# Last stage of an attention, expert and feed-forward kernel: accumulator bank by step, a lag of three, conversion in place, mixed pairs held in order

## The chip, the cores and the metric

The kernel runs on one core of a Trainium2 chip. The metric is the device time of one execution, in microseconds; the time before is the median of three runs, 920.2 us (919.64 to 920.55). One further execution was taken with the hardware profiler. Its rows name the engines PE (TensorE, matmuls), PEld (its weight loads), DVE (VectorE), ACT (ScalarE), POOL (GpSimd) and SP (SyncE, which issues most DMAs).

## The reference

Three layers follow each other on 2304 tokens of width 512. Cut to what matters:

```python
out = attention(q, k, v)                 # (4, 8, 576, 64): downsampled by 4, plus a local band of |i - j| < 4
x = out as (2304, 512)
e = argmax(x @ w_gate + bias[modality])  # one of 8 experts per token
x[e == k] = gate * (relu(x[e == k] @ w1[k]) @ w2[k])        # 512 -> 1024 -> 512
h = x @ w_in                             # 512 -> 2048
g = max(h, 0) + log1p(exp(-abs(h)))      # softplus
result = g @ w_out                       # 2048 -> 512
```

The large products need more than one pass: each operand is split into a high part (`h`) and the rest (`l`), and one product is three matmuls, high x high, high x low and low x high (`mm3`). The weights w_in and w_out arrive as 64-bit words and are converted on the chip first.

## The kernel before

Tokens are on 18 tiles of 128. After the attention, `slots` runs the experts: a slot is 128 tokens of one expert, and for each slot `gemm1` makes x @ w1, `h_t` transposes the hidden values (L1149) and splits them (L526 on ScalarE, L527 on VectorE), `gemm2` makes h @ w2. Slots 9 and 15 (of those executed) are mixed: their two halves of 64 tokens belong to two experts, and `mmx` (L561) issues for each weight slice two matmuls of half width, one for each half, with the weights `wh` and `wl` of the two experts. TensorE can run such a pair side by side. Weights come by DMA into the tiles raw0 to raw7, and ScalarE (L332) and VectorE (L333) split them.

The conversion of w_in and w_out lies beside this work. `conv_load` brings one half chunk, 512 KB, into the tile `cv` (two buffers, SyncE's queue, L188 for w_in and L191 for w_out). `conv_work` then makes 32-bit values: ScalarE scales the low words (L206, tile `cm`), VectorE shifts the high words into the tile `cy` (L209) and merges sign and the rest into `z` (L213), and GpSimd adds `cm` (L215). For the first eight chunks `z` is a tile `cz` and is stored to DRAM (`wf`), to be loaded again into a raw tile; for the last eight `z` is a half of raw4 to raw7 itself, and this runs in the last stage. `cm` and `cy` have two buffers in the slots and one in the last stage.

The last stage has 96 steps (g, c): six groups of three token tiles, sixteen chunks of 128 hidden columns. `ffn1` is the first product of a step, 12 matmuls (L552, L555, L556) into an accumulator bank `ps`, then the softplus: on ScalarE Abs (L1231, the first reader of the bank), Exp (L1232), 1 + e (L1234) and Ln (L1238), on VectorE L1237, L1239 (the last reader of the bank) and L1240, then gh (ScalarE, L1244) and gl (VectorE, L1245). `ffn2` is the second product, 9 matmuls of gh, gl with w_out into the three banks of its group, and runs LAG steps later in the program. `gather_y` (GpSimd, L1192) brings a token tile into `yg`, `y_t` transposes it (L1209), splits it (L527) and copies its index column into `ti` (VectorE, L1214).

Steps 0 to 15 are (0,0) to (0,7) and (1,0) to (1,7). Steps 16 to 21 are pairs of the two groups: (0,8), (1,8), (0,9), (1,9), (0,10), (1,10). Then (0,11) to (0,15), (1,11) to (1,15), and groups 2 to 5 in turn. The conversions of chunks 8 to 15 stand between steps 4 and 23.

The program is not executed in the order of the text: a planner with a model of the engines sets the order of every engine's queue, and only instructions marked `keep_in_program_order` keep their order among each other. Every engine works through its queue in order, each instruction behind the waits for its inputs and for free buffers.

Of the kernel before, what the change touches and what calls it, by code (L numbers as in the profile page):

```python
# [11 lines left out]
I32 = mybir.dt.int32  # L12
# [7 lines left out]
def tile_attention_moe_ffn(  # L20
# [17 lines left out]
    NT, DM = out.shape  # L38
# [31 lines left out]
    NFC = FF // 128  # L70
# [17 lines left out]
    def bank(i, shape, dt=F32):  # L88
        return psums[-1].tile(shape, dt, tag=f"p{i}", name=f"p{i}")
# [86 lines left out]
    cvp = []  # L176
# [19 lines left out]
    def conv_work():  # L196
        if cvl:
# [6 lines left out]
            m = cvp[-1].tile([128, DM], I32, tag="cm", name="cm")  # L204
            y = cvp[-1].tile([128, DM], I32, tag="cy", name="cy")
            i1 = act.activation(out=m, in_=low.bitcast(U32), func=ACTF.Copy, scale=2.0 ** -29)  # L206
            if c >= CD:
                tc.keep_in_program_order(i1)
            i1 = dve.tensor_scalar(out=y, in0=h, scalar1=3, scalar2=0x3FFFFFFF,  # L209
                              op0=ALU.logical_shift_left, op1=ALU.bitwise_and)  # L210
            if c >= CD:
                tc.keep_in_program_order(i1)
            dve.scalar_tensor_tensor(out=z, in0=h, scalar=-0x40000000, in1=y,  # L213
                                     op0=ALU.bitwise_and, op1=ALU.bitwise_or)
# [342 lines left out]

    def mmx(ps, L, R, first, last):
        for a in range(2):
            ph = slice(64 * a, 64 * a + 64)  # L560
            pe.matmul(out=ps[ph], lhsT=L[:, ph], rhs=R[a], start=first, stop=last)  # L561

# [570 lines left out]
    def phase_cd():  # L1133
# [4 lines left out]
        fpl = []  # L1138
# [37 lines left out]
        OB = 2  # L1176
        GB = 4
        GN = GT * 128
# [40 lines left out]

        def ffn1(g, c):  # L1220
            yh, yl = yT[g]
            wh, wl = split[FF0 + c]
            ps = bank(c % 2, [128, GN])
            for kc in range(KC):
# [15 lines left out]
            dve.tensor_tensor(out=e, in0=e, in1=u, op=ALU.add)  # L1240
            gp = (fpl[1], GB) if g == len(groups) - 1 and c >= NFC - GB else (fp, 3)
            gh = gp[0].tile([128, GN], F32R, tag="gh", name="gh", bufs=gp[1])
# [122 lines left out]
        for f in acts[-1]:  # L1365
            f()
        LAG = 2
        LAST = 6
        for i in range(len(steps) + LAG):
            if i < len(steps):  # L1370
                early_ = i < 4 * CD - 4
                if not early_:
                    for f in acts[i]:
                        f()
                ffn1(*steps[i])
                if early_:
                    for f in acts[i]:
                        f()
# [48 lines left out]
```

## Time and profile before

| | |
|---|---|
| median of three runs | 920.2 us |
| the profiled execution | 925.12 us, of which its span 923.4 us |
| TensorE busy | 853.3 us, 92% of the span |
| VectorE busy | 654.7 us, 71% |
| ScalarE busy | 547.1 us, 59% |
| GpSimd busy | 214.8 us, 23% |

The attention ends at about 205 us, the slots at about 490 us, and the last stage fills the rest. The share of TensorE is a mean over these: in most of the last stage it is busy without a break, and the idle time sits in the attention, at the seam to the last stage, and in single waits. So the timeline has to be read by stage, and for each wait the bracket at the end of its row says how long the engine stood and what ended it.

### The profile page before, as it was taken

Reading aid. Unit: us, or ns where it says so; the run is one execution under the profiler, and the core shown is the slowest. Engines: PE = TensorE matmul, PEld = TensorE weight load, DVE = VectorE, ACT = ScalarE, POOL = GpSimd, SP = SyncE. Lnnn points to the kernel's source line nnn. Section 1 sums busy time; section 2 is a strip of 40 time slices with the busy share of each in tenths; the row PEclk is TensorE's granted clock in tenths of the full one; section 3 lists DMA queues with packets and bytes.
Section 4 is the critical chain, followed back from the end, with each engine's and each line's share of the span. In section 5 each row is a group of like instructions: output and inputs, shape, how many; then the busy total and the mean of one; then the engine's idle time right before and its main releaser. Section 6 shows DMA issues by size and latency. Waiting matters only on the chain. (4 is left out here: it accounts for less than half of the span.)

```text
span 923.4 us, 15325 instructions
## 1 busy us (share of the span) xinstructions
PE 853.3 (92%) x5356; PEld 725.9 (79%) x5356; DVE 654.7 (71%) x1271; ACT 547.1 (59%) x935; POOL 214.8 (23%) x263
## 2 busy tenths in 40 slices
PE   6797899868899999999999999899999999999996
PEld 6687788756777766786687898789899998999984
DVE  6576487678699988976857798656656665666662
ACT  3553564453699777876857677656545555455451
POOL 8322554230243342511001222202000000000001
PEclk9998899799999999999999999999999999999999
DMA  9999785672934599577354333202001001000000
GB/s 164 191 174 195 171 199 126 177 194 94 309 123 138 175 368 332 205 265 252 115 194 147 99 94 109 69 12 65 27 12 35 23 12 34 24 12 12 24 1 34
DMA packets 109112, 115.68 MB, mean 125 GB/s; under 512 B 68448, under 2 KB 83552, under 8 KB 109024
## 3 DMA queue, kind: packets, MB, share of 16 engines
q1 hardware_dynamic: 101072, 98.28, 38.0%
q0 software_dynamic: 4960, 16.28, 5.5%
q8 instruction: 44, 0.72, 0.3%
q10 hardware_dynamic: 2992, 0.04, 0.2%
q14 instruction: 44, 0.36, 0.1%
HBM read 92.93 MB, written 21.65 MB: 124 GB/s over the span
## 5 line engine op out<-in xcount | busy, mean ns | idle before, releaser
L333 DVE TENSOR_TENSOR wl<-raw,wh 128x1024 fp32r<-128x1024 f32 x152 | 187.6, 1256 | 34.8 <-ACT wh L332 31.8
L332 ACT ACTIVATE wh<-raw 128x1024 fp32r<-128x1024 f32 x152 | 159.2, 1064 | 39.8 <-DMA raw<-in_moe_w_dram 16.7
L552 PE MATMUL p<-yh,wh 128*128 128x384 f32 x384 | 131.6, 343 | 11.3 <-DVE e L1239 10.1
L556 PE MATMUL p<-yh,wl 128*128 128x384 f32 x384 | 129.4, 337 | 0.0
L555 PE MATMUL p<-yl,wh 128*128 128x384 f32 x384 | 129.3, 337 | 0.0
L552 PE MATMUL p<-wh,gh 128*128 128x512 f32 x288 | 113.8, 395 | 1.1 <-ACT gh L1244 1.1
L555 PE MATMUL p<-wl,gh 128*128 128x512 f32 x288 | 113.2, 393 | 0.0
L556 PE MATMUL p<-wh,gl 128*128 128x512 f32 x288 | 101.4, 395 | 0.1
L1238 ACT ACTIVATE u<-u 128x384 f32<-128x384 f32 x96 | 50.1, 524 | 80.1 <-DVE e L1237 80.1
L552 PEld LDWEIGHTS p<-yh,wh 128*128 128x128 f32 x384 | 72.1, 188 | 18.7 <-DVE e L1239 14.2
L1245 DVE TENSOR_TENSOR gl<-e,gh 128x384 fp32r<-128x384 f32 x96 | 57.5, 600 | 40.7 <-ACT gh L1244 39.9
L1244 ACT ACTIVATE gh<-e 128x384 fp32r<-128x384 f32 x96 | 50.1, 523 | 45.1 <-DVE e L1240 44.8
L555 PEld LDWEIGHTS p<-yl,wh 128*128 128x128 f32 x384 | 72.2, 188 | 3.0
L1231 ACT ACTIVATE e<-p 128x384 f32<-128x384 f32 x96 | 46.4, 488 | 46.3 <-PE p L556 42.8
L556 PEld LDWEIGHTS p<-yh,wl 128*128 128x128 f32 x384 | 72.1, 188 | 0.3
L1192 POOL DMA_INDIRECT yg<-ys,pos x18 | 19.1, 1060 | 216.4 <-PE p L1209 205.7
L1237 DVE SCALAR_TENSOR_TENSOR e<-u,e 128x384 f32<-128x384 f32 x96 | 55.2, 577 | 13.4 <-ACT u L1234 11.2
L556 PEld LDWEIGHTS p<-wh,gl 128*128 128x128 f32 x288 | 54.0, 188 | 12.9 <-DVE gl L1245 0.8
L552 PEld LDWEIGHTS p<-wh,gh 128*128 128x128 f32 x288 | 54.1, 188 | 10.5 <-ACT gh L1244 1.5
L1240 DVE TENSOR_TENSOR e<-e,u 128x384 f32<-128x384 f32 x96 | 55.3, 579 | 9.0 <-ACT u L1238 1.3
L555 PEld LDWEIGHTS p<-wl,gh 128*128 128x128 f32 x288 | 54.2, 188 | 8.7
L552 PE MATMUL p<-wh,hh 128*128 128x512 f32 x144 | 58.9, 409 | 1.8 <-ACT y L1170 1.5
(256 smaller groups left out, 1800.4 us busy)
## 6 DMA issues: line engine op xcount, KB each, us to landing
raw<-in_moe_w_dram SPq DMA_DIRECT2D x40, 512.0 KB
cv<-in_moe_w_in_dram SPq DMA_DIRECT2D x16, 512.0 KB
cv<-in_moe_w_out_dram SPq DMA_DIRECT2D x16, 512.0 KB
wh<-in_moe_w_dram SPq DMA_DIRECT2D x16, 512.0 KB
wl<-in_moe_w_dram SPq DMA_DIRECT2D x16, 512.0 KB
vw<-in_v_dram SPq DMA_DIRECT2D x36, 144.0 KB
ys<-y SPq DMA_DIRECT2D x20, 256.5 KB
vg<-in_v_dram SPq DMA_DIRECT2D x16, 288.0 KB
```

Of the source, the lines that this page charges most:

```text
L332: ins = (act.activation(out=hi, in_=r, func=ACTF.Copy), dve.tensor_tensor(out=lo, in0=r, in1=f32(hi), op=ALU.subtract))
L333: dve.tensor_tensor(out=lo, in0=r, in1=f32(hi), op=ALU.subtract))
L552: i = pe.matmul(out=ps, lhsT=lh, rhs=rh, start=first, stop=False)
L555: pe.matmul(out=ps, lhsT=lh, rhs=rl, start=False, stop=False)
L556: pe.matmul(out=ps, lhsT=ll, rhs=rh, start=False, stop=last)
L1192: pool.indirect_dma_start(out=y, out_offset=None, in_=ys[0:rows], in_offset=bass.IndirectOffsetOnAxis(ap=pos[:, t:t + 1], axis=0))
L1231: act.activation(out=e, in_=ps, func=ACTF.Abs)
L1237: dve.scalar_tensor_tensor(out=e, in0=u, scalar=-1.0, in1=e, op0=ALU.add, op1=ALU.subtract)
L1238: act.activation(out=u, in_=u, func=ACTF.Ln)
L1240: dve.tensor_tensor(out=e, in0=e, in1=u, op=ALU.add)
L1244: act.activation(out=gh, in_=e, func=ACTF.Copy)
L1245: dve.tensor_tensor(out=gl, in0=e, in1=f32(gh), op=ALU.subtract)
```

## The change

There are four edits. The first product's bank is i % 2 with i the number of the step, where it was c % 2; the two differ only in some of steps 17 to 26. LAG is 3, where it was 2, with gh and gl in four buffers (were three), and GB is 3 (was 4), the number of last steps whose gh and gl have their own pool. In `conv_work` the tile `cy` is gone: the shifted high words are written straight into `z`, and the merge reads `z` and writes it. In `mmx` the half-width matmuls are marked to keep the program's order.

```diff
--- before.py
+++ after.py
@@ -202,15 +202,14 @@
             else:
                 z = raws[4 + c % 4][:, j * DM:(j + 1) * DM].bitcast(I32)
             m = cvp[-1].tile([128, DM], I32, tag="cm", name="cm")
-            y = cvp[-1].tile([128, DM], I32, tag="cy", name="cy")
             i1 = act.activation(out=m, in_=low.bitcast(U32), func=ACTF.Copy, scale=2.0 ** -29)
             if c >= CD:
                 tc.keep_in_program_order(i1)
-            i1 = dve.tensor_scalar(out=y, in0=h, scalar1=3, scalar2=0x3FFFFFFF,
+            i1 = dve.tensor_scalar(out=z, in0=h, scalar1=3, scalar2=0x3FFFFFFF,
                               op0=ALU.logical_shift_left, op1=ALU.bitwise_and)
             if c >= CD:
                 tc.keep_in_program_order(i1)
-            dve.scalar_tensor_tensor(out=z, in0=h, scalar=-0x40000000, in1=y,
+            dve.scalar_tensor_tensor(out=z, in0=h, scalar=-0x40000000, in1=z,
                                      op0=ALU.bitwise_and, op1=ALU.bitwise_or)
             pool.tensor_tensor(out=z, in0=z, in1=m, op=ALU.add)
             if c < CD:
@@ -556,9 +555,10 @@
         pe.matmul(out=ps, lhsT=ll, rhs=rh, start=False, stop=last)
 
     def mmx(ps, L, R, first, last):
+
         for a in range(2):
             ph = slice(64 * a, 64 * a + 64)
-            pe.matmul(out=ps[ph], lhsT=L[:, ph], rhs=R[a], start=first, stop=last)
+            tc.keep_in_program_order(pe.matmul(out=ps[ph], lhsT=L[:, ph], rhs=R[a], start=first, stop=last))
 
     def gemm1(s):
         for _ in gemm1_steps(s):
@@ -1174,7 +1174,7 @@
 
         GT = 3
         OB = 2
-        GB = 4
+        GB = 3
         GN = GT * 128
         groups = [list(range(t, t + GT)) for t in range(0, NTT, GT)]
 
@@ -1217,10 +1217,10 @@
         def acc(g):
             return 2 + 3 * (g % 2)
 
-        def ffn1(g, c):
+        def ffn1(i, g, c):
             yh, yl = yT[g]
             wh, wl = split[FF0 + c]
-            ps = bank(c % 2, [128, GN])
+            ps = bank(i % 2, [128, GN])
             for kc in range(KC):
                 sl = slice(kc * 128, (kc + 1) * 128)
                 mm3(ps, (wh[:, sl], wl[:, sl]), (yh[:, kc, :], yl[:, kc, :]), kc == 0, kc == KC - 1)
@@ -1238,7 +1238,7 @@
             act.activation(out=u, in_=u, func=ACTF.Ln)
             dve.scalar_tensor_tensor(out=e, in0=ps, scalar=0.0, in1=e, op0=ALU.max, op1=ALU.subtract)
             dve.tensor_tensor(out=e, in0=e, in1=u, op=ALU.add)
-            gp = (fpl[1], GB) if g == len(groups) - 1 and c >= NFC - GB else (fp, 3)
+            gp = (fpl[1], GB) if g == len(groups) - 1 and c >= NFC - GB else (fp, 4)
             gh = gp[0].tile([128, GN], F32R, tag="gh", name="gh", bufs=gp[1])
             gl = gp[0].tile([128, GN], F32R, tag="gl", name="gl", bufs=gp[1])
             act.activation(out=gh, in_=e, func=ACTF.Copy)
@@ -1364,7 +1364,7 @@
                 acts[at + 1].append(lambda c=CD + i // 2: split_part(FF0 + c))
         for f in acts[-1]:
             f()
-        LAG = 2
+        LAG = 3
         LAST = 6
         for i in range(len(steps) + LAG):
             if i < len(steps):
@@ -1372,7 +1372,7 @@
                 if not early_:
                     for f in acts[i]:
                         f()
-                ffn1(*steps[i])
+                ffn1(i, *steps[i])
                 if early_:
                     for f in acts[i]:
                         f()
```

Since `cy` is a line less, lines 206 to 556 of before have a number one lower after it: L209, L213, L333 and L527 are L208, L212, L332 and L526, and in the order below L551, L554, L555 are the three matmuls of a product.

**VectorE, the start of the last stage.** The names are e (the softplus of a step, one number for each step), p0 and p1 (the two banks), gl, wl (a weight's low part) and ti. Before, behind the first product's L1237 of step 2:

```order
L1237 SCALAR_TENSOR_TENSOR e_6996<-u_6997,e_6996 128x384
L1240 TENSOR_TENSOR e_6955<-e_6955,u_6956 128x384
L1239 SCALAR_TENSOR_TENSOR e_6996<-p0_6983,e_6996 128x384
L1240 TENSOR_TENSOR e_6996<-e_6996,u_6997 128x384
L1245 TENSOR_TENSOR gl_6965<-e_6955,gh_6964 128x384
L333 TENSOR_TENSOR wl_6969<-raw5_87,wh_6968 128x1024
L1245 TENSOR_TENSOR gl_7006<-e_6996,gh_7005 128x384
L333 TENSOR_TENSOR wl_7010<-raw6_88,wh_7009 128x1024
L527 TENSOR_TENSOR yl_6973<-p6_7057,yh_6972 128x4x128
L1214 CAST ti_8134<-yg_7504 128x1
```

The first conversion stands 20 rows further down:

```order
L1240 TENSOR_TENSOR e_7088<-e_7088,u_7089 128x384
L527 TENSOR_TENSOR yl_6973<-p7_7144,yh_6972 128x4x128
L1245 TENSOR_TENSOR gl_7098<-e_7088,gh_7097 128x384
L209 TENSOR_SCALAR cy_7102<-cv_6904 128x512
L1237 SCALAR_TENSOR_TENSOR e_7131<-u_7132,e_7131 128x384
L213 SCALAR_TENSOR_TENSOR raw4_86<-cv_6904,cy_7102 128x512
```

Now, from the same place, L1237 of step 2:

```order
L1237 SCALAR_TENSOR_TENSOR e_6980<-u_6981,e_6980 128x384
L1214 CAST ti_7125<-yg_6997 128x1
L208 TENSOR_SCALAR raw4_86<-cv_6890 128x512
L1240 TENSOR_TENSOR e_6939<-e_6939,u_6940 128x384
L1239 SCALAR_TENSOR_TENSOR e_6980<-p0_6967,e_6980 128x384
L212 SCALAR_TENSOR_TENSOR raw4_86<-cv_6890,raw4_86 128x512
L1240 TENSOR_TENSOR e_6980<-e_6980,u_6981 128x384
L1245 TENSOR_TENSOR gl_6949<-e_6939,gh_6948 128x384
L332 TENSOR_TENSOR wl_6953<-raw5_87,wh_6952 128x1024
L526 TENSOR_TENSOR yl_6957<-p6_7029,yh_6956 128x4x128
L1245 TENSOR_TENSOR gl_6990<-e_6980,gh_6989 128x384
L332 TENSOR_TENSOR wl_6994<-raw6_88,wh_6993 128x1024
```

A first conversion operation (L208, on cv_6890, the load of w_out that SyncE issues as the second of the two) has moved up, ahead of L1240 of step 1 and L1239 of step 2; the other half's conversion (cv_6888) stands 20 rows behind it.

**TensorE, the part of the pairs.** p0 and p1 are the first product's banks, p2 to p7 those of the second products; yh_5299 is group 0 and yh_6972 group 1. Before, from the last matmul of step (1,8) to the first two of (0,10):

```order
L556 MATMUL p0_7652<-yh_6972,wl_7197 128x384
L552 MATMUL p2_7015<-wh_7196,gh_7631 128x512
L555 MATMUL p2_7015<-wl_7197,gh_7631 128x512
L552 MATMUL p3_7016<-wh_7196,gh_7631 128x512
L555 MATMUL p3_7016<-wl_7197,gh_7631 128x512
L552 MATMUL p4_7017<-wh_7196,gh_7631 128x512
L555 MATMUL p4_7017<-wl_7197,gh_7631 128x512
L556 MATMUL p2_7015<-wh_7196,gl_7632 128x512
L556 MATMUL p3_7016<-wh_7196,gl_7632 128x512
L556 MATMUL p4_7017<-wh_7196,gl_7632 128x512
L552 MATMUL p0_7785<-yh_5299,wh_7414 128x384
L555 MATMUL p0_7785<-yl_5300,wh_7414 128x384
```

Now, from the last matmul of step (1,9) to the first two of (0,10), which is p0_7746 there:

```order
L555 MATMUL p1_7702<-yh_6956,wl_7258 128x384
L551 MATMUL p5_7391<-wh_7169,gh_7638 128x512
L554 MATMUL p5_7391<-wl_7170,gh_7638 128x512
L551 MATMUL p6_7392<-wh_7169,gh_7638 128x512
L554 MATMUL p6_7392<-wl_7170,gh_7638 128x512
L551 MATMUL p7_7393<-wh_7169,gh_7638 128x512
L554 MATMUL p7_7393<-wl_7170,gh_7638 128x512
L555 MATMUL p5_7391<-wh_7169,gl_7639 128x512
L555 MATMUL p6_7392<-wh_7169,gl_7639 128x512
L555 MATMUL p7_7393<-wh_7169,gl_7639 128x512
L551 MATMUL p0_7746<-yh_5290,wh_7380 128x384
L554 MATMUL p0_7746<-yl_5291,wh_7380 128x384
```

Before, two first products of bank 0 had one second product between them, and now the first products of this part alternate between the banks.

**TensorE, slot 15's second product.** p_5568 before and p_5556 after are its accumulator. Before, the last pairs and the transposes behind them:

```order
L561 MATMUL p5_5568<-wh_5456,hh_5470 64x512
L289 UNCONDITIONAL_BRANCH
L561 MATMUL p5_5568<-wl_5458,hh_5470 64x512
L561 MATMUL p5_5568<-wh_5456,hh_5470 64x512
L561 MATMUL p5_5568<-wl_5458,hh_5470 64x512
L1149 MATMUL p3_5615<-ident_70,h_5483 128x128 x4
L289 UNCONDITIONAL_BRANCH
L1149 MATMUL p4_5622<-ident_70,h_5483 128x128 x4
L289 UNCONDITIONAL_BRANCH
```

Now:

```order
L561 MATMUL p5_5556<-wh_5445,hh_5459 64x512
L1149 MATMUL p3_5603<-ident_70,h_5472 128x128 x2
L288 UNCONDITIONAL_BRANCH
L561 MATMUL p5_5556<-wl_5447,hh_5459 64x512
L561 MATMUL p5_5556<-wh_5445,hh_5459 64x512
L288 UNCONDITIONAL_BRANCH
L561 MATMUL p5_5556<-wl_5447,hh_5459 64x512
L1149 MATMUL p3_5603<-ident_70,h_5472 128x128 x2
L1149 MATMUL p4_5610<-ident_70,h_5472 128x128
```

The last pairs now have transposes of the next slot's hidden values between their two halves.

## Rows read from the trace of the kernel before

**Rows 1.** Busy us (x instructions) by stretch: PE, PEld, DVE, ACT, POOL; PEclk; DMA
```profile
650.00:700.00 50.00, 50.00 (x256) 45.06 (x256) 32.03 (x64) 25.03 (x50) 3.47 (x3) 1.00 0.06 18
```

**Rows 2.** Timeline of TensorE, late last stage: start, us, engine, line, operation, [wait]
```profile
887.25 0.34 PE L552 MATMUL p<-yh,wh 128*128 128x384 f32 x1
...
889.37 0.39 PE L552 MATMUL p<-wh,gh 128*128 128x512 f32 x1
...
891.45 0.33 PE L552 MATMUL p<-yh,wh 128*128 128x384 f32 x1
```

**Rows 3.** Timeline of TensorE, the part of alternating pairs
```profile
574.36 0.45 PE L552 MATMUL p<-yh,wh 128*128 128x384 f32 x1 [1.66 <-DVE e L1239]
...
584.74 0.44 PE L552 MATMUL p<-yh,wh 128*128 128x384 f32 x1 [1.72 <-DVE e L1239]
...
622.63 0.44 PE L552 MATMUL p<-yh,wh 128*128 128x384 f32 x1 [1.69 <-DVE e L1239]
```

**Rows 4.** Busy time by stretch, one of those waits
```profile
574.00:575.00 1.00, 0.64 (x4) 0.64 (x5) 1.00 (x3) 0.40 (x1) 0.00 (x0) 1.00 0.47 163
```

**Rows 5.** Timeline of VectorE, start of the last stage
```profile
502.22 0.55 DVE L1240 TENSOR_TENSOR e<-e,u 128x384 f32<-128x384 f32 x1
502.69 0.55 DVE L1239 SCALAR_TENSOR_TENSOR e<-p,e 128x384 f32<-128x384 f32 x1
...
507.06 0.68 DVE L527 TENSOR_TENSOR yl<-p,yh 128x512 fp32r<-128x512 f32 x1
511.15 0.15 DVE L1214 CAST ti<-yg 128x1 int32<-128x1 f32 x1 [3.40 <-DMA yg<-ys,pos]
...
517.35 0.42 DVE L209 TENSOR_SCALAR cy<-cv 128x512 int32<-128x512 int32 x1
```

**Rows 6.** Timeline of TensorE, start of the last stage
```profile
504.44 0.42 PE L552 MATMUL p<-yh,wh 128*128 128x384 f32 x1
...
512.43 0.44 PE L552 MATMUL p<-yh,wh 128*128 128x384 f32 x1 [1.49 <-DVE e L1239]
```

**Rows 7.** Timeline of SyncE's DMA issues, start of the last stage
```profile
491.77 12.35 SPq L272 DMA_DIRECT2D raw<-wf  x4
...
505.01 0.44 SPq L191 DMA_DIRECT2D cv<-in_moe_w_out_dram  x1
```

**Rows 8.** DMA queues from 510 to 511: packets, MB, share of 16 engines
```profile
q1 hardware_dynamic: 22, 0.06, 15.3%
```

**Rows 9.** VectorE by line and form: busy us, mean ns | idle before
```profile
L333 DVE TENSOR_TENSOR wl<-raw,wh 128x1024 fp32r<-128x1024 f32 x152 | 187.6, 1256 | 34.8 <-ACT wh L332 31.8 <-DMA wh<-in_moe_w_dram 2.3
L1245 DVE TENSOR_TENSOR gl<-e,gh 128x384 fp32r<-128x384 f32 x96 | 57.5, 600 | 40.7 <-ACT gh L1244 39.9
...
L213 DVE SCALAR_TENSOR_TENSOR cz<-cv,cy 128x512 int32<-128x512 int32 x16 | 12.3, 768 | 0.2
```

**Rows 10.** Timeline of TensorE, slots stage
```profile
384.39 0.80 PE L556 MATMUL p<-wh,hl 128*128 128x512 f32 x1 [2.04 <-DVE hl L527]
```

**Rows 11.** Busy time by stretch, behind that wait
```profile
385.00:386.00 1.00, 1.00 (x4) 0.81 (x3) 1.00 (x2) 0.25 (x1) 0.98 (x1) 0.50 0.28 109
387.00:388.00 1.00, 1.00 (x4) 0.77 (x4) 1.00 (x2) 0.56 (x1) 1.00 (x1) 0.62 0.67 172
```

**Rows 12.** Timeline of TensorE, slot 9's second product, and slot 15's end
```profile
357.87 0.59 PE L561 MATMUL p<-wh,hh 128*64 128x512 f32 x1
...
358.30 0.59 PE L561 MATMUL p<-wh,hh 128*64 128x512 f32 x1
...
358.82 1.10 PE L1149 MATMUL p<-ident,h 128*128 128x128 f32 x7
...
363.27 0.51 PE L555 MATMUL p<-wl,xh 128*128 128x512 f32 x1
...
445.77 1.22 PE L1149 MATMUL p<-ident,h 128*128 128x128 f32 x8
...
447.07 0.39 PE L555 MATMUL p<-wl,xh 128*128 128x512 f32 x1
```

## The prediction

> **What bounds the kernel now.** Start with the busy time by stretch. In a stretch of the last stage without disturbance TensorE is busy 50.00 of 50 us with 256 matmuls, while VectorE has 32 us of work [rows 1]. So the last stage is bound by TensorE wherever nothing holds it, and a change can only win where it waits. The timeline of TensorE gives the unit: a first product (12 matmuls) lasts 2.12 us, from 887.25 to 889.37, and a second product (9 matmuls) 2.08 us, to 891.45 [rows 2]. Next look for bracketed waits in that timeline. In the part where pairs of steps alternate between two token groups there are four of one kind, each ended by VectorE's L1239, the last reader of the accumulator bank: 1.66, 1.72, 1.72 and 1.69 us [rows 3] (the third repeats the second and is not shown). The last thing to see is the start of the stage, where VectorE sits in a wait of 3.40 us until 511.15 and TensorE's next first product starts at 512.43 after 1.49 us of waiting [rows 5, 6].
>
> **The bank of the first product.** In the old order the bank is c % 2, so the two steps of a pair share a bank, and two first products of one bank come nearly next to each other: p0_7652 (step (1,8)), one second product, p0_7785 (step (0,10)), as the order of TensorE above shows. The second must wait for the chain ACT L1231, L1232, L1234, DVE L1237, L1239 of the first. The four waits sum to 1.66 + 1.72 + 1.72 + 1.69 = 6.79 us. The first matmul after a wait also stands 0.44 us instead of 0.34 [rows 2, 3], so four restarts give 4 x 0.11, about 0.45 more. In the new order the same steps run bank 0, second product, bank 1, second product: between the end of a first product and the next use of its bank lie second + first + second product, 2.08 + 2.12 + 2.08 = 6.28 us, as in the undisturbed stretch, where nothing waits. The waits ended after 2.08 + 1.66 = 3.74 us where one second product lay between, so 6.28 us covers that chain. Term A: **-7.2 us** (bounds -7.3 and, if one of the four is kept, -5.4). The clock plays no part: during such a wait it is still 1.00 [rows 4].
>
> **The lag of three.** Executed second products were ordered by the planner, and in the undisturbed stretch both orders have the second product of two steps ago behind each first product. The extra gh/gl pair therefore buys nothing there: 0. At the end of the kernel the order is the same, GB of 3 included: 0. In the early steps new double placements arise; step 12's first product follows the last use of its bank by 5.4 us instead of 6.3 (one first product, 2.12, and 14 second-product matmuls of 0.23 by the order). The chain took 3.74 us in one place, and 4.16 + 1.72 = 5.88 where two second products lay between and VectorE was late [rows 3]. So 0 to 0.5; I take **+0.3**. The transposes of the third to fifth gathered tile also move among the second products; a wait for a gather lies between 0 and the 3.40 seen in [rows 5]; I take **+0.2**, because the gathers are issued 10 us and more ahead.
>
> **The conversion in place.** The tile cy had one buffer, and with it the planner kept the first conversion of the last stage late, at 517.35 [rows 5]. Without it the planner pulls one up: L208 on cv_6890 now stands in VectorE's queue ahead of L1240 of step 1 and L1239 of step 2 (the order of VectorE above). cv_6890 is the second conversion load. SyncE's order is unchanged: of four loads of wf the last one goes out late, with 12.35 us over the group, then the two conversion loads, the second at 505.01 [rows 7]. The queue of these loads still moves 22 packets after 510 us [rows 8], so it lands at about 511.0. VectorE executes in order. So it stands from about 502.3 (where L1240 ran at 502.22) to 511.0, instead of working until 507.74 and waiting then to 511.15 [rows 5]. Behind it queue L1239, which frees bank 0, and gl of steps 1 and 2; TensorE has one first product and transposes left and then nothing: step 4, which began at 504.44, begins after L208, L1240 and L1239, 0.42 + 0.55 + 0.55 = 1.5 us behind the landing, at 512.5 [rows 5, 6]. TensorE thus idles 504.4 to 512.5, 8.1 us.
> After that, step 5 (at 512.43 before) must follow step 4 and two second products: 2.12 + 2.08 + 2.08 = 6.28 us, so 518.8 at full clock. VectorE's own queue to the L1239 that frees its bank is L208 0.42, L1240 0.55, L1239 0.55, L212 0.77, L1240 0.55, L1245 0.60, L332 1.26, L526 0.68, L1245 0.60, L332 1.26, the cast 0.15, L1237 and L1239 0.55 each, 8.5 us, so 519.5, or 518.6 with the 0.07 overlap of neighbours that the starts show [rows 5, 9]. And the clock: after an idle of 2.04 us at 384.39 it stood at 0.50 and was not back before the slice from 387 [rows 10, 11], 3.6 us at half pace, which costs 1.8 us of work. With it step 5 starts at 518.8 + 1.8 = 520.6. That is 520.6 - 512.43 = **+8.2 us**, term B. Bounds: +6.2 (VectorE alone, 518.6), and with the step and one second product all at half pace, 4.20 more, +10.6. I take the clock value, since 8.1 us of idling is far over 2.04. Nothing gives it back: behind this point both engines run as before, with TensorE full.
> The Trainium skill's page "TensorE: Matmul & The Clock Gate", section "Why this matters for your kernels", warns of idle gaps of TensorE between bursts, after which the engine is back at the lower of its clocks. The trace agrees for the gap of 2.04 us and shows none of it for 1.7 us [rows 4, 11]. Without that rule B would be +7.1, which is in the range.
> Later conversions are not hit: the loads behind are issued after the L212 before them, and over 5 us of VectorE work lie between in the new order, while TensorE is the bound. In the slots the first operation now waits for the store of two conversions before, which L213 waited for until now; its idle time was 0.2 us in 16 [rows 9]. L208 comes 0.42 earlier, so 16 x 0.42 would be the worst; I take 0, with +-1.
>
> **The mixed pairs.** Pairs of half-width matmuls run side by side: a pair starts 0.43 us after the other [rows 12]. Keeping program order does not make them adjacent everywhere. Slot 9's second product was split by transposes and stays split; from 358.82 to 363.27 it took 4.45 us for eight transposes, one L552 and four pairs; an unsplit place has transposes and L552 in 1.30, with 4 x 0.43 = 1.72 that is 3.02 [rows 12]. A split costs 1.4; two half-width matmuls run singly alone would cost 2 x 0.43 = 0.9. In the new order slot 15's second product is split by transposes as well (its order above), where TensorE sets the pace: **+1.3**. Slot 9's first product gets its pairs separated too, before a point where TensorE waits 2.04 us for VectorE [rows 10]; the delay comes off that wait. Up to 1.3 if it doesn't; if the shortened wait leaves the clock up, it gains 3.6/2 less what it took, down to -1.6. I take **-0.5**.
> The Trainium skill, "TensorEngine Tiling (Array Packing)", section "Key Properties", says that changing the tiling mode drains the engine. The 1.4 against 0.9 fits that; by 0.9 the sum would be 0.4 lower.
>
> **The sum.** -7.2 + 0.3 + 0.2 + 8.2 + 1.3 - 0.5 = +2.3 us. The profiled execution took 925.1 us (span 923.4), so 927.4 in its frame; the runs' median is 920.2, and 0.25% on it gives **922.5 us**. A measurement of this kernel tells 0.2% from nothing, 1.8 us: faster is under 918.4, slower over 922.0. Since -7.2 and +8.2 nearly cancel, the forecast of a small slowdown stands close to that bound.
>
> **The rivals.**
> *Main case*: terms as above, 922.5, in a band of 919.5 to 925.5; chance 0.58, of which 0.33 slower and 0.25 same.
> *The early conversion waits little* (not slower). If the second load lands before 507, because SyncE gets through its code sooner in the new program, VectorE's stand is 4 us shorter and B falls to +2 or less; then 920.2 - 7.2 + 1.3 + 2 = 916.3. For it: only the issue times hold that load, a single row with 12.35 us for four issues [rows 7]. Against: the order on SyncE is the same word for word, and the bytes show the queue full until 510. Chance 0.15, faster.
> *The backlog carries* (slower). TensorE stays at half pace for more than 3.6 us, and VectorE, which has conversions to do in the next 50 us, has no slack to refill; then B reaches +10.6, step 12 waits 0.5 and slot 9's split costs its 1.3 too: -7.2 + 10.6 + 0.5 + 1.3 + 1.3 + 0.2 = +6.7, 926.9. It decides if the clock is still at 0.50 when step 4 has ended. Chance 0.13.
> *The wait at 384 goes* (not slower). Slot 9's split is taken off the wait of 2.04 us and the clock stays up behind it, -1.6 instead of -0.5, and VectorE's shifted order in the slots gives up to 1 us more: 920.2 + 2.3 - 1.1 = 921.4, down to 920.4. With B at its lower bound too, 6.2, it is 918.4. Chance 0.14, of which 0.08 same and 0.06 faster.
>
> **How the numbers follow.** Faster: 0.15 + 0.06 = 0.21. Slower: 0.33 + 0.13 = 0.46. Same: 0.25 + 0.08 = 0.33. The range 916 to 926.5 holds the main case, the third rival and most of the first; it leaves out the worst of the second and the best of the first.
>
> **What would show it.** A: no bracketed wait of 1.7 us by L1239 in the timeline of TensorE at steps 16 to 28. B: in VectorE's timeline one bracketed wait of some 8 us on the load of cv before L208 at about 511 us, TensorE's step 4 first matmul with an idle of 8 us, and slices of 0.50 behind it. Mixed pairs: lone L561 rows near slots 9 and 15 with transposes between. Wrong would be: the L208 with no wait (then the time is 916), or four waits still there under other steps (then 929).

## The result

The changed kernel takes 925.34 us (median of 22 runs, 920.17 to 928.17) and the kernel before 920.08 in runs beside it (22, 912.76 to 924.27). The ratio is 1.0052, 95% interval 1.0034 to 1.0070: 4.8 us slower (3.1 to 6.5). The forecast was slower by 2.3 us, 922.5, with a range of 916 to 926.5.

The two profiled executions differ by less, 925.1 us of span against 923.4. Most of what is missing lies ahead of everything that the change touches, in the attention: up to the first expert product the twelve traces told of here differ by up to 4.2 us (203.50 to 207.71), whatever the kernel. So all that follows goes by stages, cut at first matmuls that each kernel has: the first expert product (at 207.03 in the kernel before), the eight transposes behind the wait of [rows 10] (391.14), the first product of step 0 (491.75) and of step 33 (640.28). In the changed kernel these rows of TensorE's timeline are:

```profile
204.37 0.78 PE L551 MATMUL b<-wh,xh 128*128 128x512 f32 x1
...
391.02 1.12 PE L1149 MATMUL p<-ident,h 128*128 128x128 f32 x8
...
493.98 0.45 PE L551 MATMUL p<-yh,wh 128*128 128x384 f32 x1 [1.10 <-ACTq L1324]
...
642.06 0.34 PE L551 MATMUL p<-yh,wh 128*128 128x384 f32 x1
```

The lengths of the stages in us, with those of the experiments told of below:

| kernel | to the first expert product | to the transposes | to step 0 | to step 33 | to the end |
|---|---|---|---|---|---|
| before | 207.03 | 184.11 | 100.61 | 148.53 | 283.12 |
| before again (e8) | 205.13 | 183.87 | 100.61 | 148.05 | 283.14 |
| **after** | 204.37 | 186.65 | 102.96 | 148.08 | 283.04 |
| e1 bank alone | 204.82 | 182.35 | 100.59 | 142.00 | 283.14 |
| e2 in place alone | 206.97 | 185.27 | 100.59 | 156.69 | 283.08 |
| e3 kept pairs alone | 206.80 | 182.15 | 102.95 | 147.55 | 283.15 |
| e4 after, anchored | 207.71 | 186.39 | 102.93 | 139.79 | 282.98 |
| e5 after, three cz | 203.50 | 184.54 | 102.96 | 147.09 | 283.01 |
| e6 all mended | 204.45 | 182.41 | 100.60 | 140.84 | 283.00 |
| e7 after, lag 2 | 204.30 | 186.82 | 102.93 | 146.37 | 283.08 |
| e9 in place, anchored | 206.27 | 186.06 | 100.59 | 147.85 | 283.13 |
| e10 mended, lag 2 | 206.56 | 183.73 | 100.61 | 140.92 | 283.08 |

The changed kernel loses 2.5 to 2.8 us up to the transposes and 2.35 from there to step 0. From step 0 to step 33 it comes out even, and behind it nothing differs.

Each row of the table is one execution. How much that leaves open is seen on the kernel before, e8 and e1: their engines have the same order in the slots, and up to the transposes they take 184.11, 183.87 and 182.35. All three have the wait of [rows 10] (2.04, 2.11 and 2.09 us); behind it TensorE's clock fell to 0.50 in the first two and stayed at 1.00 in e1.

**The start of the last stage.** VectorE's timeline of the changed kernel, which answers to [rows 5]: the early conversion stands on its load.

```profile
503.84 0.55 DVE L1237 SCALAR_TENSOR_TENSOR e<-u,e 128x384 f32<-128x384 f32 x1
504.31 0.15 DVE L1214 CAST ti<-yg 128x1 int32<-128x1 f32 x1
512.11 0.43 DVE L208 TENSOR_SCALAR raw<-cv 128x512 int32<-128x512 int32 x1 [7.65 <-DMA cv<-in_moe_w_out_dram]
512.45 0.55 DVE L1240 TENSOR_TENSOR e<-e,u 128x384 f32<-128x384 f32 x1
512.92 0.55 DVE L1239 SCALAR_TENSOR_TENSOR e<-p,e 128x384 f32<-128x384 f32 x1
```

The bracket names the load of w_out and 7.65 us. L1240 and L1239 of the softplus follow within 0.8 us, as soon as the queue moves. On TensorE, against [rows 6], step 4 starts behind an idle time of 6.84 us, and step 5, the last row, at 522.72:

```profile
503.98 0.44 PE L551 MATMUL p<-yh,wh 128*128 128x384 f32 x1 [0.31 <-DVE e L1239]
...
513.62 0.66 PE L551 MATMUL p<-yh,wh 128*128 128x384 f32 x1 [6.84 <-ACT gh L1244]
...
517.59 0.63 PE L551 MATMUL p<-wh,gh 128*128 128x512 f32 x1
...
522.72 0.34 PE L551 MATMUL p<-yh,wh 128*128 128x384 f32 x1
```

The bracket says ACT gh. The row also needs its bank, and VectorE's L1239 of 512.92, which frees it, ends at 513.47, 0.15 ahead of the row; gh is only what the profile saw last, and both stood behind the same L208. Step 4 lasts from 513.62 to 517.59, 3.97 us instead of 2.12 [rows 2], and the two second products behind it 5.13 instead of 4.16. The reason is the clock. In the busy times by stretch it is the number behind POOL's, 0.50 until the slice from 519:

```profile
516.00:517.00 1.00, 1.00 (x5) 1.00 (x5) 1.00 (x3) 0.97 (x3) 0.00 (x0) 0.50 0.00 0
...
519.00:520.00 1.00, 1.00 (x5) 0.78 (x4) 0.96 (x3) 0.97 (x3) 0.00 (x0) 0.66 0.00 0
520.00:521.00 1.00, 1.00 (x6) 0.83 (x5) 1.00 (x3) 0.70 (x3) 0.00 (x0) 1.00 0.00 0
```

SyncE's issues, against [rows 7]: the group of four loads of wf is again drawn out, over 9.56 us, and the second conversion load goes out at 505.12. L208 starts 7 us later, at 512.11.

```profile
493.99 9.56 SPq L271 DMA_DIRECT2D raw<-wf  x4
...
505.12 0.43 SPq L191 DMA_DIRECT2D cv<-in_moe_w_out_dram  x1
```

**The pairs of steps.** The four waits of [rows 3] are gone. From 570 to 640 TensorE is busy throughout, where it was 63.22 of 70 us. Busy times by stretch, before and after:

```profile
570.00:640.00 70.00, 63.22 (x318) 55.96 (x317) 44.60 (x83) 44.01 (x90) 14.84 (x12) 1.00 0.17 53
```

```profile
570.00:640.00 70.00, 70.00 (x357) 63.11 (x356) 53.95 (x93) 49.01 (x99) 15.86 (x14) 1.00 0.21 68
```

**The slots.** This is what the prediction did not have. In VectorE's timeline the first conversion operation waits for a store of wf: three L208 rows of one stretch, and between them the last work (L526, until 364.56) ahead of the longest stand:

```profile
360.94 0.62 DVE L208 TENSOR_SCALAR cz<-cv 128x512 int32<-128x512 int32 x1 [0.73 <-DMA wf<-cz]
...
363.29 1.27 DVE L526 TENSOR_TENSOR hl<-p,hh 128x512 fp32r<-128x512 f32 x2
369.21 0.43 DVE L208 TENSOR_SCALAR cz<-cv 128x512 int32<-128x512 int32 x1 [4.65 <-DMA wf<-cz]
...
373.91 0.43 DVE L208 TENSOR_SCALAR cz<-cv 128x512 int32<-128x512 int32 x1 [1.40 <-DMA wf<-cz]
```

The store it needs at 369.21 is that of two conversions before, and SyncE issued it at 361.31. So from the issue of the store to the release of the row it took 7.9 us. From 364 to 370 us the queue of loads and stores filled the 16 DMA engines:

```profile
361.31 0.33 SPq L216 DMA_DIRECT2D wf<-cz  x1
```

```profile
q1 hardware_dynamic: 952, 2.06, 100.6%
```

Behind the standing VectorE, TensorE stands for 3.94 us, waiting for xl. This is another place than that of [rows 10], which waited for hl in the next product; that wait is gone here. The clock falls as it did there [rows 11]:

```profile
377.87 1.22 PE L555 MATMUL p<-wh,xl 128*128 128x512 f32 x2 [3.94 <-DVE xl L526]
378.89 0.63 PE L551 MATMUL p<-wh,xh 128*128 128x512 f32 x1
```

Matmuls of 512 columns then start 0.42 us apart, where they start 0.23 apart at the full clock.

### The profile page after: what moved, and what is told of

Read it like the earlier page. It is cut to its first block, busy times and chain, and to the rows that moved or that the text cites. A ratio compares the mean times of both kernels' runs of the same rounds, so it can differ in the third digit from the quotient of the medians.

```text
span 925.1 us, 15302 instructions
## 1 busy us (share of the span) xinstructions
PE 859.8 (93%) x5356; PEld 730.7 (79%) x5356; DVE 655.3 (71%) x1271; ACT 549.3 (59%) x935; POOL 219.3 (24%) x263
## 5 line engine op out<-in xcount | busy, mean ns | idle before, releaser
L332 DVE TENSOR_TENSOR wl<-raw,wh 128x1024 fp32r<-128x1024 f32 x152 | 188.6, 1265 | 32.8 <-ACT wh L331 29.7
L551 PE MATMUL p<-yh,wh 128*128 128x384 f32 x384 | 131.9, 343 | 9.6 <-ACT gh L1244 6.8
L555 PE MATMUL p<-yh,wl 128*128 128x384 f32 x384 | 130.2, 339 | 0.0
L554 PE MATMUL p<-yl,wh 128*128 128x384 f32 x384 | 130.1, 339 | 0.0
L551 PE MATMUL p<-wh,gh 128*128 128x512 f32 x288 | 114.3, 397 | 1.1 <-ACT gh L1244 1.1
L554 PE MATMUL p<-wl,gh 128*128 128x512 f32 x288 | 113.8, 395 | 0.0
L555 PE MATMUL p<-wh,gl 128*128 128x512 f32 x288 | 104.7, 395 | 0.0
L1245 DVE TENSOR_TENSOR gl<-e,gh 128x384 fp32r<-128x384 f32 x96 | 55.4, 577 | 42.0 <-ACT gh L1244 39.5
L551 PEld LDWEIGHTS p<-yh,wh 128*128 128x128 f32 x384 | 72.7, 189 | 15.4 <-ACT gh L1244 7.1
L554 PEld LDWEIGHTS p<-yl,wh 128*128 128x128 f32 x384 | 72.8, 190 | 3.3
L555 PEld LDWEIGHTS p<-yh,wl 128*128 128x128 f32 x384 | 72.7, 189 | 0.0
L1240 DVE TENSOR_TENSOR e<-e,u 128x384 f32<-128x384 f32 x96 | 57.8, 602 | 9.7 <-ACT u L1238 1.5
L555 PEld LDWEIGHTS p<-wh,gl 128*128 128x128 f32 x288 | 54.0, 188 | 12.6 <-DVE gl L1245 0.3
L551 PEld LDWEIGHTS p<-wh,gh 128*128 128x128 f32 x288 | 54.5, 189 | 10.6 <-ACT gh L1244 1.5
L1237 DVE SCALAR_TENSOR_TENSOR e<-u,e 128x384 f32<-128x384 f32 x96 | 55.1, 574 | 10.5 <-ACT u L1234 8.4
L554 PEld LDWEIGHTS p<-wl,gh 128*128 128x128 f32 x288 | 54.6, 190 | 9.1
L555 PE MATMUL p<-wh,xl 128*128 128x512 f32 x136 | 54.1, 410 | 6.9 <-DVE xl L526 6.9
```

Of the source, the lines that this page charges most:

```text
L332: dve.tensor_tensor(out=lo, in0=r, in1=f32(hi), op=ALU.subtract))
L551: i = pe.matmul(out=ps, lhsT=lh, rhs=rh, start=first, stop=False)
L554: pe.matmul(out=ps, lhsT=lh, rhs=rl, start=False, stop=False)
L555: pe.matmul(out=ps, lhsT=ll, rhs=rh, start=False, stop=last)
L1237: dve.scalar_tensor_tensor(out=e, in0=u, scalar=-1.0, in1=e, op0=ALU.add, op1=ALU.subtract)
L1245: dve.tensor_tensor(out=gl, in0=e, in1=f32(gh), op=ALU.subtract)
```

## The experiments

Lengths of stages are those of the table above; a ratio is to the kernel before, run beside it on the same chip, with its 95% interval. Each edit is to the kernel before in e1, e2, e3 and e9 and to the changed kernel in e4 to e7 and e10.

**e1: the bank alone.**

```diff
-        def ffn1(g, c):
+        def ffn1(i, g, c):
-            ps = bank(c % 2, [128, GN])
+            ps = bank(i % 2, [128, GN])
```

> The kernel before with one edit only, the first product's bank by step. TensorE's and VectorE's queues are as before up to step 16. Theory 1 (the four bank waits are the change's only gain, and nothing comes late in their place): 7 to 8 us less than before, about 912.5, ratio 0.992, no wait of 1.7 us left. Theory 2 (the gain seen in the changed kernel's trace was VectorE catching up after its earlier stand, not the banks): less than 3 us gained, with new waits on L1239 between steps 16 and 28.

Measured: 915.02 us against 921.21, ratio 0.9947 (0.9920 to 0.9973), 4.9 us less. From step 0 to 33 it is 142.00 instead of 148.05 to 148.53, 6.0 to 6.5 less. Of this, 5.6 lies behind step 5 (122.20 from step 5 to 33 instead of 127.81 to 127.85), where the banks are. The rest is mostly a shorter wait at step 5, the first row below; that wait differs from trace to trace without the edit too (1.49 and 1.18 us in the kernel before, 0.79 in e3). So Theory 1 has the cause, but its 7 to 8 us do not all come: three of the four waits went, and one of 1.57 us stayed, the only long wait of TensorE between 510 and 640 us.

```profile
507.56 0.45 PE L552 MATMUL p<-yh,wh 128*128 128x384 f32 x1 [0.65 <-DVE e L1239]
...
578.14 0.44 PE L552 MATMUL p<-yh,wh 128*128 128x384 f32 x1 [1.57 <-DVE e L1239]
```

**e2: the conversion in place alone.**

```diff
-            y = cvp[-1].tile([128, DM], I32, tag="cy", name="cy")
-            i1 = dve.tensor_scalar(out=y, in0=h, scalar1=3, scalar2=0x3FFFFFFF,
+            i1 = dve.tensor_scalar(out=z, in0=h, scalar1=3, scalar2=0x3FFFFFFF,
-            dve.scalar_tensor_tensor(out=z, in0=h, scalar=-0x40000000, in1=y,
+            dve.scalar_tensor_tensor(out=z, in0=h, scalar=-0x40000000, in1=z,
```

> The kernel before with one edit only, the conversion in place. The planner again pulls the second conversion of the last stage up, here even one row of step 1 further. Theory 1 (the conversion in place costs the stand on the load at the start of the last stage, some 8 us, and in the slots the waits of L208 for a store, some 2.5 us): 9 to 12 us more than before, about 930. Theory 2 (the waits for stores in the slots are off the path and the loss there comes from the pairs): 7 to 9 us more, about 928, and the slots end as early as before.

Measured: 932.86 against 921.21, ratio 1.0134 (1.0103 to 1.0166), 12.3 us more. The load is waited for 8.12 us, and since the conversion stands a row of step 1 further up, TensorE idles 9.19 us:

```profile
510.76 0.43 DVE L208 TENSOR_SCALAR raw<-cv 128x512 int32<-128x512 int32 x1 [8.12 <-DMA cv<-in_moe_w_out_dram]
```

```profile
511.71 0.69 PE L551 MATMUL p<-yh,wh 128*128 128x384 f32 x1 [9.19 <-DVE e L1238]
```

Up to the transposes it takes 185.27, 1.2 and 1.4 above the two traces of the kernel before. In this trace the clock stayed at 1.00 behind its waits there, of 2.01 and 2.03 us; against the traces that also kept it (e1 182.35, e3 182.15) it is 3.0 more. Theory 1 stands on both counts.

**e3: the pairs kept in order alone.**

```diff
-            pe.matmul(out=ps[ph], lhsT=L[:, ph], rhs=R[a], start=first, stop=last)
+            tc.keep_in_program_order(pe.matmul(out=ps[ph], lhsT=L[:, ph], rhs=R[a], start=first, stop=last))
```

> The kernel before with one edit only, the half-width matmuls kept in program order. Theory 1: slot 15's second product is split (1.2 us), slot 9's splits are absorbed by VectorE: 1 to 2.5 us more than before, about 922. Theory 2 (the loss in the slots up to 391 us comes from the split pairs): 4 to 5 us more, about 925. Theory 3 (kept order makes pairs adjacent and gains): 1 us less.

Measured: 922.75 against 921.21, ratio 1.0018 (0.9993 to 1.0044), which alone decides nothing. The stages do: 102.95 instead of 100.61 from the transposes to step 0, the same 2.35 as in the changed kernel, and 182.15 ahead of it, so nothing is seen to be lost at slot 9. Theory 1. Of the 2.35, 1.2 is the split of slot 15's second product. In the changed kernel:

```profile
439.79 0.64 PE L561 MATMUL p<-wh,hh 128*64 128x512 f32 x1
...
448.98 0.48 PE L551 MATMUL p<-wh,xh 128*128 128x512 f32 x1
```

From its first pair to the product behind the transposes it takes 9.19 us, and unsplit it took 8.00 (438.75 to 446.75). The other 1.1 comes ahead of it: with the kept order the planner puts the second product of the slot before ahead of slot 15's first one, where its weights are not split yet, and takes the transposes apart in two groups:

```profile
417.09 1.04 PE L1209 MATMUL p<-ident,yg 128*128 128x128 f32 x8
...
419.88 0.50 PE L555 MATMUL p<-wh,hl 128*128 128x512 f32 x1 [0.64 <-DVE wl L332]
...
425.63 0.64 PE L561 MATMUL p<-wh,xh 128*64 128x512 f32 x1
...
433.54 0.48 PE L551 MATMUL p<-wh,xh 128*128 128x512 f32 x1
```

From 417.09 to 433.54 it is 16.45 us, and was 15.38 (417.18 to 432.56); the wait of 0.64 is the larger part of the difference.

**e4: the changed kernel with the conversion anchored.** The reading behind this run is that the mark that keeps an instruction in order ties it to the instruction that was written last on its engine. For the second conversion that would be the index copy of a gathered tile (L1214), which the planner can do early, and L208 does stand right behind one in the changed kernel. Put ahead of the transposes of its step, the conversion would be tied to that step's softplus. The run shows the order that comes out, not the rule itself.

```diff
-            acts[at].append(conv_work)
+            acts[at].insert(0, conv_work)
```

> The changed kernel with the conversion put ahead of the transposes among the work of its step, so that the mark that holds it in order ties it to the softplus of step 5 and not to the early index copy. The planner then leaves the first conversions behind step 4, the rest of the order is nearly that of the changed kernel. Theory 1 (the stand on the load costs 8 us): 7.5 to 9 us less than the changed kernel, about 917, with VectorE's wait of 7.65 us gone. Theory 2 (another wait takes its place, since gathers and loads land at 511 whatever VectorE does): 2 us less or nothing.

Measured: 917.66 against 921.21, ratio 0.9962 (0.9937 to 0.9986), so 0.9% or 8.3 us under the changed kernel. From step 0 to 33 it is 139.79 instead of 148.08, also 8.3: step 5 comes 9.7 us sooner behind step 0 (19.04 instead of 28.74), and 1.4 is lost again up to step 33 (120.75 instead of 119.34), where bank waits of 0.28 and 0.77 us are back. Theory 1: VectorE's longest wait in that place is now 1.82 us, for a gather.

```profile
514.78 0.15 DVE L1214 CAST ti<-yg 128x1 int32<-128x1 f32 x1 [1.82 <-DMA yg<-ys,pos]
```

The waits for stores in the slots are there unchanged:

```profile
371.46 0.43 DVE L208 TENSOR_SCALAR cz<-cv 128x512 int32<-128x512 int32 x1 [3.89 <-DMA wf<-cz]
```

**e5: the changed kernel with three buffers for cz.**

```diff
-                z = cvp[-1].tile([128, DM], I32, tag="cz", name="cz")
+                z = cvp[-1].tile([128, DM], I32, tag="cz", name="cz", bufs=3)
```

> The changed kernel with three buffers for cz, so that the first conversion operation in the slots needs the store of three conversions ago, not of two. In the last stage the order is the changed kernel's. Theory 1 (the waits of L208 for stores cost the time from the first expert product to the transposes at 391 us, 186.4 us in three traces with the conversion in place against 182.2 without): 182 to 184 there, 2.5 to 4 us less than the changed kernel, about 922. Theory 2 (what is lost there comes from slot 9's split pairs and the half clock behind a wait, not from the stores): waits gone, but 185 or more from the first product to the transposes, and at most 1 us less in all.

Measured: 922.43 against 920.47, ratio 1.0009 (0.9987 to 1.0032), 0.4% under the changed kernel's ratio. To the transposes it takes 184.54, 2.1 less than the changed kernel, a little more than the 182 to 184 expected, but Theory 1 and not Theory 2. No row of VectorE waits for a store any more; the conversion's first operation waits for its loads, as it did before:

```profile
DVE cz L208 <- DMA cv<-in_moe_w_in_dram: 2.5, 2, 1.9
```

**e6: the changed kernel with three mends**, the diffs of e4 and e5 and `mmx` as it was.

> The changed kernel with three mends: conversion ahead of the transposes among its step's work, three buffers for cz, half-width matmuls not kept in order. The bank by step and the lag of three stay. If the parts add up: 8.3 less for the stand on the load, 2.5 to 4 for the stores, 2.4 for slot 15, so 13 to 15 us less than the changed kernel, 910.5 to 912.5, and 4 us under the kernel with the bank alone. If they overlap (one wait replaced by another): 915 or more, no better than the bank alone.

Measured: 912.36 against 920.47, ratio 0.9900 (0.9862 to 0.9938). The parts add up, and this kernel is 0.6 to 1.4% faster than the kernel before. That it is 4 us under the bank alone is not shown: its interval overlaps that of e1, and from the first expert product on the two traces differ by 1.2 us. Two of its longer waits, one of a bank and the one ahead of the transposes:

```profile
576.72 0.44 PE L551 MATMUL p<-yh,wh 128*128 128x384 f32 x1 [1.30 <-DVE e L1239]
```

```profile
380.08 0.54 PE L555 MATMUL p<-wh,hl 128*128 128x512 f32 x1 [1.92 <-DVE hl L526]
```

**e7: the changed kernel with a lag of two**, LAG, GB and the buffers of gh and gl as before.

> The changed kernel with a lag of two, three buffers for gh and gl, and four last steps. The order is the changed kernel's up to step 5. My prediction put the lag at 0 to +0.5 us. Theory 1 (the lag does nothing): same as the changed kernel within 0.5 us, and from step 5 to step 33 some 119.3 us. Theory 2 (the lag with its buffers is what removes the last of the bank waits, since the kernel with the bank alone kept one of 1.57 us and took 122.2 us from step 5 to 33): one wait of 1.5 us at step 21 or 22 again, about 122 from step 5 to 33, and 2 to 3 us more than the changed kernel.

Measured: 926.90 against 920.47, ratio 1.0072 (1.0049 to 1.0094). That is not apart from the changed kernel's. A bank wait came back, as Theory 2 had it, but at 1.08 us:

```profile
588.79 0.44 PE L551 MATMUL p<-yh,wh 128*128 128x384 f32 x1 [1.08 <-DVE e L1239]
```

From step 5 to 33 it takes 120.45, 1.1 more than the changed kernel's 119.34. But from step 0 to 33 it is 146.37, less than the changed kernel, because step 5 came 2.8 us sooner: its load was there 16.6 us behind step 0 and not 18.1, and the clock was back at 1.00 sooner (below). So this run alone does not settle the lag.

**e8: the kernel before once more.**

> The kernel before once more, for a second profile. Theory 1 (the wait of 2.04 us at 384 us and the half clock behind it in the first profile are a matter of the single execution): 182.2 to 182.5 us from the first expert product to the transposes at 391, as in the two kernels whose slots have the same conversions, instead of 184.1. Theory 2 (they belong to the kernel): 184 again.

Measured, in a single execution: 183.87 us to the transposes, with the wait of [rows 10] again. The wait belongs to the kernel, as Theory 2 has it: it stands in all three traces with this order of the slots. The half clock behind it does not in the same way: e1 has the wait without it, and is the shorter one.

```profile
382.23 0.50 PE L556 MATMUL p<-wh,hl 128*128 128x512 f32 x1 [2.11 <-DVE hl L527]
```

**e9: the kernel before, in place and anchored**, the diffs of e2 and e4.

> The kernel before with the conversion in place and the conversion ahead of the transposes among its step's work, so that no conversion is pulled up at the start of the last stage. What is left of the conversion in place is the waits for stores in the slots. Theory 1 (these waits cost some 3 us): 185.5 to 187 us from the first expert product to the transposes at 391, about 3 us more than the kernel before, ratio 1.003, and the last stage as in the kernel before. Theory 2 (without the kept half-width order the waits are absorbed): 183 to 184 there and no change in all.

Measured: 924.06 against 921.70, ratio 1.0023 (1.0004 to 1.0042), 2.1 us more. To the transposes it is 186.06, and the last stage is the kernel before's, 147.85. Theory 1, at 2.0 to 2.2 instead of 3. Against e2 (156.69) the early conversion costs 8.8 us.

**e10: the mended kernel with a lag of two.**

> The kernel with three mends, with a lag of two, three buffers for gh and gl, and four last steps. Theory 1 (the lag is worth 1 us, as 120.45 against 119.34 us from step 5 to 33 said): 913 to 914, a wait of 1 to 1.6 us at step 21 to 23. Theory 2 (the lag is worth the whole 2.8 us by which the kernel with the bank alone was longer there): 915, as the bank alone. Theory 3 (nothing): 912.4.

Measured: 913.53 against 921.70, ratio 0.9907 (0.9885 to 0.9928). From step 0 to 33 it is 140.92, against 140.84 in e6. Theory 3: in the mended kernel the lag of three with its buffers is worth nothing that these runs can tell.

## Why the prediction was right, and where it was not

**What bounds the kernel, and the tail.** As read: TensorE, with nothing gained or lost behind step 33 (283.04 against 283.12 and 283.14). The direction of the forecast and its range held. That the sum came as near as 2.5 us is in part luck: the terms of the slots were 4.1 us too low and those of the last stage 2.0 too high, as the rest of this section shows.

**The banks (A, -7.2).** Right in the mechanism, and a little small. In the changed kernel all four waits went, and from step 5 to 33 it takes 119.34 us instead of 127.85, 8.5 less for the same matmuls. Of the 1.3 above the forecast 7.2, some 0.7 is in how the wait was read. The bracket counts from the end that the profile gives the matmul before, 582.62 + 0.40 in the rows below; but the next matmul would have started 0.23 us behind its start, where these matmuls follow each other without a wait.

```profile
582.39 0.40 PE L555 MATMUL p<-wl,gh 128*128 128x512 f32 x1
582.62 0.40 PE L556 MATMUL p<-wh,gl 128*128 128x512 f32 x1
584.74 0.44 PE L552 MATMUL p<-yh,wh 128*128 128x384 f32 x1 [1.72 <-DVE e L1239]
```

From start to start it is 2.12 where 0.23 is usual, so this wait cost 1.89 and not 1.72, and the four with their restarts 7.9. The remaining 0.6 lies in smaller pieces that were not followed. How many bank waits stay depends on the order around them. Alone the edit gave 5.6 from step 5 to 33 (e1), and 6.3 between e9 and e10; e1, e4, e6 and e7 each kept a wait of 0.8 to 1.6 us. The prediction took all four as gone, which was right for this kernel.

**The lag (0, +0.3 and +0.2).** The 0.5 us of loss did not come: from step 5 to 33 the changed kernel's TensorE has no wait at all. In the mended kernel the lag is worth nothing (e10). In the changed kernel a lag of two brings a bank wait back and takes 1.1 us more from step 5 to 33 (e7), so there the lag seems to gain a little.

**The early conversion (B, +8.2).** The mechanism and the size were right: step 5 lies 28.74 us behind step 0 instead of 20.68, +8.06, and the two pairs of kernels with and without it differ by 8.3 and 8.8 up to step 33. Inside, two errors cancel. The load landed 18.1 us behind step 0, where 19.3 was taken, so the idle time was 6.84 and not 8.1. And the half clock lasted longer: it cost 3.97 - 2.12 + 5.13 - 4.16 = 2.8 us, where 1.8 was taken from the wait at 384. That nothing gives the time back behind that point is nearly right: against e4 the changed kernel is 9.7 us behind at step 5 and 8.3 at step 33.

**The mixed pairs (+1.3 - 0.5).** The split of slot 15 was sized right, 1.2. What failed is the step that looked at the mixed products alone: the mark also changed what the planner put around them, and that cost 1.1 more. Slot 9's -0.5 is not to be seen: with the pairs alone (e3) the wait of [rows 10] did shrink, to 1.72 us, with the clock at 1.00 behind it, but e1, without the pairs, kept the clock too and is as long up to the transposes (182.35 against 182.15).

**The stores in the slots (0, +-1).** This is the step that failed. The seven traces without the conversion in place or with three cz take 182.15 to 184.54 us up to the transposes, mean 183.3; the five with it and two cz take 185.27 to 186.82, mean 186.2. That is +2.9. It is there whether or not the clock fell behind the waits near 380 us: where it fell the means are 183.7 and 186.5, where it did not 182.25 and 185.27 (one trace). The runs that differ by this alone, compared singly, give 1.2 to 2.2 (e2 and e9 against the kernel before, e5 against the changed one), so the size is known to about 1 us. The prediction read rightly that L213 hardly waited, 0.2 us in 16 [rows 9], but took the time by which the new wait comes earlier as the length of L209, 0.42. Between L209 and its L213 the planner had put weight splits of other work, so the real distance is longer, as the kernel before shows in its timeline of VectorE:

```profile
369.23 0.54 DVE L209 TENSOR_SCALAR cy<-cv 128x512 int32<-128x512 int32 x1 [0.90 <-DMA cv<-in_moe_w_out_dram]
...
370.82 0.68 DVE L213 SCALAR_TENSOR_TENSOR cz<-cv,cy 128x512 int32<-128x512 int32 x1
```

So the write into `cz` came 1.59 us later than L209, nearly four times 0.42, and in the other four conversions from 359 to 382 us it came 1.59 to 3.78 later. In that time VectorE did L333 and other work. In place, the same wait stands at the head of the pair, and everything behind it stands too. A wait for a buffer has to be costed from the row that waits for it, back to the row that would now wait, with all that the queue does between them.

**The sum.** +2.3 was forecast. By the stages of the two profiles it is (186.65 - 184.11) + (102.96 - 100.61) + (148.08 - 148.53) + (283.04 - 283.12) = +4.4, and with e8 in place of the first profile +5.1; the runs say 4.8. Stage by stage, with the last one cut at step 5:

| stage | forecast | measured, first profile | why |
|---|---|---|---|
| to the transposes | -0.5 | +2.54 | the stores; slot 9's gain not seen |
| to step 0 | +1.3 | +2.35 | the order around slot 15 |
| step 0 to 5 | +8.2 | +8.06 | two errors that cancel |
| step 5 to 33 | -7.2 + 0.5 = -6.7 | -8.51 | banks 1.3 more, no loss by the lag |
| behind | 0 | -0.08 | |

So the first two stages were forecast 4.1 us too low, and the last stage 2.0 too high. Why the changed kernel and e5 have no bank wait left behind step 5 where the others have one is shown in part: they alone have the early conversion, the bank by step and the lag of three together, and without the early conversion (e4) or with a lag of two (e7) one is back.

**The rivals.** The early conversion waited, so the first rival fell. For the second, the backlog that carries, its sign came and its price did not: the clock was still at 0.50 when step 4 had ended at 517.59, yet B was +8.06 and not +10.6, and no wait followed behind step 5. For the third, the wait for hl at 384 did go, but another of 3.94 us, for xl, stands ahead of it with the half clock behind.

## To carry to other kernels

A buffer that looks like waste can be what holds an instruction back: before one is removed, see in the order of the queue what it kept late, and keep the instruction behind the work that it must follow. A write in place moves the wait for its target from the second operation to the first; if stores are slow there, that wait holds the whole in-order queue. And a mark that keeps some instructions in order can change where the planner puts others, so compare the rows around them and not the marked ones alone.

## What the runs showed that was not expected

A store of 256 KB took 7.9 us from issue to release while the DMA engines were full (100.6% by the queue's row).

TensorE's clock was at half not only behind 6.84 and 3.94 us of idling: it was at 0.50 behind 1.92 us in e6 (the wait at 380.08 above).

```profile
381.00:382.00 1.00, 1.00 (x4) 0.81 (x3) 1.00 (x2) 0.06 (x1) 1.00 (x1) 0.50 0.61 240
```

But the length of the wait alone does not tell. The clock stayed at 1.00 behind the waits of 1.6 to 1.7 us at the banks, and also behind 2.09 us in e1, behind 2.01 and 2.03 in e2, and behind 2.36 us in the kernel before. The rows, first of the kernel before and then of e1:

```profile
221.02 1.23 PE L1149 MATMUL p<-ident,h 128*128 128x128 f32 x8 [2.36 <-DVE xl L527]
222.00:223.00 1.00, 1.00 (x7) 0.84 (x6) 0.56 (x1) 0.89 (x2) 0.00 (x0) 1.00 1.00 385
```

```profile
381.94 0.50 PE L556 MATMUL p<-wh,hl 128*128 128x512 f32 x1 [2.09 <-DVE hl L527]
383.00:384.00 1.00, 1.00 (x6) 0.82 (x5) 1.00 (x2) 0.84 (x1) 1.00 (x1) 1.00 0.68 262
```

The prediction had read the waits of 2.04 and 1.7 us alone, which look as if they had a limit between them. Which waits near 2 us bring the half clock is not known from these runs, and it is one reason why a stage of a single trace should not be read to the last microsecond.

How long half pace lasted also differed: some 3.4 us from the first matmul in the kernel before, 3.2 in e7 behind a wait of 5.28 us, and from 513.62 into the slice from 519 in the changed one, 5.4 us and more. The 1.8 us for the half clock in the prediction's B, taken from a single wait, was one value of a spread.
